# Earlier column sums, grouped weight differences and earlier x transfers in a fused cross-attention and expert layer

## The chip, the cores and the metric

The kernel runs on one core of one Trainium2 chip. The metric is device time in microseconds (us); a run that the measurement labels slow is kept out of every comparison. Engines are named as in the profile: PE (TensorE, matmuls), DVE (VectorE), ACT (ScalarE), POOL (GpSimd) and SP (SyncE, which issues transfers). Starts and landings are counted from the start of the profiled span.

## The reference

Eight batches, each of 8 heads, 512 rows of x and 32 rows of state with 64 columns, go through a cross attention in both directions; the 544 x 512 result of a batch goes through a two-layer network with 2048 hidden columns.

```python
scores = x @ state^T / 8;   a  = softmax(scores);   xread = a @ state
scores2 = state @ x^T / 8;  a2 = softmax(scores2);  sread = a2 @ x
y = concatenate([xread, sread], rows)          # heads side by side: 4352 x 512
h = y @ w_in                                   # 4352 x 2048
r = maximum(h, 0);  g = s * r*r + b            # s and b are single numbers
out = g @ w_out                                # 4352 x 512
```

## The kernel before

Step s of the main loop computes the hidden layer of batch s in 16 pieces f, and between them the output matmuls of batch s-1, the attention of batch s+1 and the transfers for later batches. In the names of the code and the profile, h is the hidden layer before its relu and g after its square, o (or oA, oB, oC by bank) the output, T the scores from the transposed x, xT that transpose, wsum the column sums; qa and u are what DVE reads out of banks A and B, and osb is a finished block of output. The output of batches 1 to 7 is made by a seven-product scheme in half-size blocks: its products read differences of weight blocks (`wd`) and sums of token blocks (`s`), and collect in three banks A, B and C. The constant b enters as b times the column sums of w_out; these sums are made once, in step 1.

```python
def bias_sum():                                  # column sums of w_out
    ps = att_ps([P, DM], FP32, "wsum_ps")
    ...                                          # 16 matmuls in tiles of 32 columns
    nc.vector.tensor_copy(wsum[:, 0], ps)
    nc.vector.tensor_sub(wsum[:, 1], ps, wsum[:, 0])

def bias_end():                                  # PE reads wsum here
    for i in range(2):
        mm(ps2, mean16, wsum[:, i], start=(i == 0), stop=(i == 1))
    ...

# the order of the seven products of the last batch: (product, from step, to step)
if b == last_b:
    order = [(1, 0, 8), (6, 0, 4), (2, 0, 2), (6, 4, 8), (2, 2, 5)]
    order += [(7, 0, 8), (2, 5, 8), (4, 0, 8)]
...
if s == 1:                                       # what step 1 does beside its matmuls
    ...
    at(8, lambda: att_xT_dma(3))                 # transpose of x of batch 3, by transfer
    at(12, lambda: load_x(4))
    at(3, bias_sum)                              # after the fourth h
    at(4, bias_end)
    ...
if 2 < s < B - 2:
    at(0, lambda: load_x(s + 2))
...
for f in range(NKF):
    mm1_x(s, f)                                  # the h of piece f: 2 matmuls, relu, square
    ...
    for fn in todo_s.get(f, []):
        fn()
    if (s == 1 and 5 <= f < 12) or (s == 2 and f == 6):
        with tc.issue_after(G["last"]):
            sums.pop(0)()                        # one weight difference
```

PE, SP and POOL run in the order written; DVE and ACT are scheduled. The transpose of batch 3 stands in a chain of transfers: the load of x of batch 3 waits on POOL for the transpose of batch 2, and the transpose of batch 3 waits for that load.

The softmax here doesn't subtract the row's maximum and nothing guards it: scores larger than these inputs give would overflow.

Of the kernel before, what the change touches and what calls it, by code (L numbers as in the profile page):

```python
# [14 lines left out]
def kernel(  # L15
# [15 lines left out]
    B, H, S, D = x.shape  # L31
# [81 lines left out]
    def new_xn(b):  # L113
        xn[b] = xpool.tile([P, H, SCH, D], FP16, name=f"xn_{b}", tag="xn", bufs=5)
# [3 lines left out]
    def load_x(b):  # L118
        new_xn(b)
        nc.gpsimd.dma_start(  # L120
            out=xn[b].rearrange("p h c d -> p h (c d)"),
            in_=x[b].rearrange("h (q c) d -> q h (c d)", q=P),
        )
# [48 lines left out]
    def new_xT(b):  # L172
        A[b]["xT"] = apool.tile([P, H, 2, P], FP16, name=f"xT_{b}", tag="xT")
        return A[b]["xT"]
# [27 lines left out]
    def att_xT_dma(b):  # L202
        xT = new_xT(b)
        nc.sync.dma_start_transpose(
            out=xT.rearrange("p h k t -> p (h k) t"),
            in_=xn[b].rearrange("p h c d -> p (h c d)"),
        )
# [46 lines left out]
    def att_shares(b):  # L254
        a = A[b]
        by_slot = "p j (q s) -> p (j q) s"
        den = apool.tile([P, NG * SCH * NQ], FP32, name=f"den_{b}", tag="den", bufs=1)
        inv = apool.tile([P, NG * SCH * NQ], FP16, name=f"inv_{b}", tag="inv", bufs=1)
        a["aT"] = apool.tile([P, NG * SCH, P], FP16, name=f"aT_{b}", tag="R", bufs=1)
        ET_s = a["ET"].rearrange(by_slot, q=NQ)  # L260
        with tc.issue_after(G["last"]):
            nc.vector.reduce_sum(den, ET_s, axis=mybir.AxisListType.X)
            with nc.allow_low_precision("shares are fp16"):
                nc.vector.reciprocal(inv, den)
            nc.vector.tensor_mul(
                a["aT"].rearrange(by_slot, q=NQ),
                ET_s,
                inv.unsqueeze(2).broadcast_to([P, NG * SCH * NQ, Ns]),
            )

    def att_a4_dma(b):
        a = A[b]
        a["a4"] = apool.tile([P, NG, S], FP16, name=f"a4_{b}", tag="a4")
        nc.sync.dma_start_transpose(
            out=a["a4"].rearrange("p g (c t) -> p (g c) t", c=SCH),
            in_=a["aT"].rearrange("t j p -> t (j p)"),
        )
# [27 lines left out]
    def att_ET(b):  # L305
        a = A[b]
        a["ET"] = apool.tile([P, NG * SCH, P], FP16, name=f"ET_{b}", tag="ET", bufs=3)
        nc.sync.dma_start_transpose(out=a["ET"], in_=a["E"].rearrange("p g t -> p (g t)"))
        a["rq"] = apool.tile([P, NG], FP32, name=f"rq_{b}", tag="rq", bufs=4)
        nc.vector.reciprocal(a["rq"], a["rs"])  # L310
# [41 lines left out]
    def mm1_open(key, ntok, f):  # L352
        pool, tag = psH, "h"
        if key == 0 and f % 2 == 1:
            pool, tag = (psA, "att") if f < 8 else (psH, "h")
        return pool.tile([P, ntok], FP32, tag=tag, name=f"h_{key}_{f}")
# [17 lines left out]
    def mm1_k(b, f, g, hps):  # L374
        a = A[b]
        mm(
            hps,
            a["M"][:, g, P * f : P * f + P],
            a["a4"][:, g, :],
            start=(g == 0),  # L380
            stop=(g == NG - 1),
        )

    def mm1_x(b, f):
        hps = mm1_open(b, S, f)
        for g in range(NG):
            mm1_k(b, f, g, hps)
        mm1_close(b, hps, S, f)
# [86 lines left out]
    def fast_items(b):  # L475
# [119 lines left out]
        order = [(1, 0, 8), (6, 0, 4), (2, 0, 3), (6, 4, 8), (2, 3, 8), (7, 0, 8)]  # L595
        order += [(5, 0, 8), (4, 0, 8), (3, 0, 8)]
        if b == last_b:
            order = [(1, 0, 8), (6, 0, 4), (2, 0, 2), (6, 4, 8), (2, 2, 5)]
            order += [(7, 0, 8), (2, 5, 8), (4, 0, 8)]
        if b == "sr":  # L600
            order = [(p, 0, 8) for p in (1, 6, 2, 7, 5, 4, 3)]
        out = [(p, k, i) for p, k0, k1 in order for k in range(k0, k1) for i in range(ni)]
# [57 lines left out]
    with tc.manual_schedule(engines={ET.PE, ET.SP, ET.Pool}):  # L660
# [90 lines left out]
        def pieces(s):  # L751
            nb = s + 1
            out = {}

            def at(f, fn):
                out.setdefault(f, []).append(fn)

            if s == 1:
                at(0, lambda: att_xT_dma(2))
                at(0, gated_x3)  # L760
                at(0, lambda: att_ET(0))
                at(0, lambda: att_ET(1))
                at(8, lambda: att_xT_dma(3))
                at(12, lambda: load_x(4))
                at(2, lambda: att_M(1, 2, "act"))
                at(3, bias_sum)
                at(4, bias_end)
                at(3, lambda: att_M(1, 3, "act"))
                at(6, lambda: att_stT(2))
                at(10, bias_half)  # L770
                at(8, lambda: att_M(2, 0, "act"))
                at(8, lambda: att_M(2, 1, "act"))
                at(10, lambda: att_M(2, 2, "act"))
                at(10, lambda: att_T(2, [0, 1]))
                at(11, lambda: att_ET(2))
                at(12, lambda: att_D(2, [0, 1]))
                at(13, lambda: att_M(2, 3, "act"))
                at(13, lambda: att_V(0))
                return out
            if 2 < s < B - 2:  # L780
                at(0, lambda: load_x(s + 2))
            if nb < NST:
                at(0, lambda: att_stT(nb))
            if nb < B:
                at(3, lambda: att_T(nb, [0, 1]))
                at(3, lambda: att_M(nb, 0, "act"))
                at(4, lambda: att_ET(nb))
                at(8, lambda: att_shares(nb))
                at(9, lambda: att_a4_dma(nb))
                if s == 3:  # L790
                    at(9, stT_dma)
                if nb + 1 < B:
                    at(9, lambda: att_xT_dma(nb + 1))
                at(7, lambda: att_M(nb, 1, "act"))
                at(7, lambda: att_M(nb, 2, "act"))
            if s == 2:
                at(1, lambda: att_srT_dma(0))
                at(8, lambda: att_V(1))
                at(12, lambda: att_srT_dma(1))
            at(10, lambda: att_V(s))  # L800
            if s == last_b:
                at(11, lambda: att_srT(s))
            else:
                at(12, lambda: att_srT_dma(s))
            if nb < B:
                at(10, lambda: att_M(nb, 3, "act"))
            if s == last_b:
                for i in range(4):
                    at(12 + i, lambda i=i: mm1_sr(i))
            return out  # L810
# [4 lines left out]
        for s in range(1, B):  # L815
            todo_s = pieces(s)
            if s in fast:
                coming[s] = fast_items(s)
            first = coming[s][:16] if s in fast else []
            if s == 1:  # L820
                items = [[] for _ in range(NKF)]
                for f in [*range(5), *range(6, 14)]:
                    items[f] = [lambda u=todo.pop(0): unit(u)]
                items[14], items[15] = first[0:8], first[8:16]
            else:
                flat = coming[s - 1][16:] + first
                n = -(-len(flat) // NKF)
                items = [flat[n * f : n * f + n] for f in range(NKF)]
            for f in range(NKF):
                mm1_x(s, f)  # L830
                if s > 1 and f in (5, 6):
                    with tc.issue_after(G["last"]):
                        token_sum(s - 1, 4, f - 5)
                if s in fast:
                    if f in ((7, 9) if s == 1 else (7, 11)):
                        with tc.issue_after(G["last"]):
                            token_sum(s, 3, f // 8)
                    if s == 1 and f in (13, 14):
                        with tc.issue_after(G["last"]):
                            token_sum(s, f - 12, 0)  # L840
                    if s > 1 and f in (11, 12):
                        token_sum(s, f - 10, 0)
                    if f == 15:
                        token_sum(s, 1, 1)
                        token_sum(s, 2, 1)
                for fn in todo_s.get(f, []):
                    fn()
                if (s == 1 and 5 <= f < 12) or (s == 2 and f == 6):
                    with tc.issue_after(G["last"]):
                        sums.pop(0)()  # L850
                for fn in items[f]:
                    fn()
# [56 lines left out]
```

## Time and profile before

| | before |
|---|---|
| time, median of three runs (lowest to highest) | 209.89 us (209.81 to 210.26) |
| span of the profiled run | 207.7 us |
| first output matmul of batch 0 starts | 23.18 us |
| T of batch 3 (scores from transposed x) starts | 56.78 us |
| last matmul starts | 203.64 us |
| transpose of x of batch 3 lands | 55.43 us |

The table cuts the span into an **opening** (23.18 us, loads and first attention), a **first stretch** up to the T of batch 3 (56.78-23.18 = 33.60), a **second stretch** up to the last matmul (203.64-56.78 = 146.86), and some 4.1 us in which the last results are read out and stored. PE leads throughout the two stretches.

### The profile page before, as it was taken

To read this page: it belongs to the slowest core of one execution; us is meant where nothing else is said; L and a number is where in the kernel's file an instruction comes from. 1 tells how busy PE (TensorE), PEld (TensorE's weight loads), DVE (VectorE), ACT (ScalarE), POOL (GpSimd) and SP (SyncE) were. 2 spreads that over 40 slices of the span, in tenths; PEclk is the share of its full clock that TensorE was granted. 3 is DMA by queue.
4 is the path that set the end of the run, shared out by engine and by line. 5 is a ranking of instruction groups with operands and counts; after the bars stand their busy time and mean duration, and the time that the engine had idled before them with its cause. 6 is when DMAs were issued, how large, how long until landed. Compare 5 with 4: busy or idle time off the path is not lost.

```text
span 207.7 us, 4765 instructions
## 1 busy us (share of the span) xinstructions
PE 199.8 (96%) x1949; PEld 129.6 (62%) x1949; DVE 162.2 (78%) x286; ACT 123.4 (59%) x216; POOL 37.6 (18%) x64
## 2 busy tenths in 40 slices
PE   7988999999999999999999999999999999999992
PEld 2424343445666676667666766676667777788881
DVE  1587825978779995999699968996899787796862
ACT  3678865698477548755776477656774545533100
POOL 5970001411110230023012201120112012100210
PEclk9999999999999999999999999999999999999999
DMA  6999996999750589269943983291314111200143
GB/s 181 227 202 206 206 192 91 192 172 180 208 67 37 125 197 133 68 78 241 141 96 96 213 110 101 80 192 44 101 58 103 50 54 50 97 7 0 55 148 106
DMA packets 46490, 25.48 MB, mean 123 GB/s; under 512 B 31428, under 2 KB 44484, under 8 KB 46468
## 3 DMA queue, kind: packets, MB, share of 16 engines
q0 software_dynamic: 15536, 16.19, 38.4%
q1 hardware_dynamic: 30132, 8.62, 23.5%
q10 hardware_dynamic: 800, 0.36, 0.7%
q8 instruction: 15, 0.25, 0.5%
q14 instruction: 7, 0.06, 0.1%
HBM read 17.33 MB, written 8.91 MB: 126 GB/s over the span
## 4 chain that ended last, share of the span: by engine, by line
PE 84%; DVE 8%; ACT 4%; issue 1%; DVEq 0%
PE h L70 23%; PE oB L70 16%; PE oC L70 11%; PE oA L70 11%; PE o L70 6%; PE Mps L70 4%; PE warm_ps L70 3%; PE h_sr L70 3%; ACT r L365 2%; DVE g L371 2%; PE T L70 1%; PE oB_sr L70 1%; PE V L70 1%; DVE M L298 1%; PE oC_sr L70 1%
## 5 line engine op out<-in xcount | busy, mean ns | idle before, releaser
L365 ACT ACTIVATE r<-h 128x512 f16<-128x512 f32 x126 | 74.5, 601 | 54.1 <-PE h L70 53.4
L70 PE MATMUL h<-a,M 128*128 128x512 f16 x256 | 75.0, 379 | 0.9 <-DVE M L298 0.6
L371 DVE TENSOR_TENSOR g<-r 128x1024 f16<-128x1024 f16 x64 | 44.1, 691 | 21.2 <-ACT r L365 21.0
L70 PEld LDWEIGHTS <-s 128*128 128x128 f16 x448 | 42.8, 98 | 19.2 <-issue 4.2
L70 PEld LDWEIGHTS <-g 128*128 128x128 f16 x400 | 38.1, 98 | 18.9 <-issue 2.9
L536 POOL DMA_DIRECT2D out_dram<-osb x27 | 18.3, 676 | 124.4 <-DVE osb L528 123.1
L70 PE MATMUL oB<-wd,s 128*128 128x256 f16 x224 | 32.7, 273 | 0.0
L70 PE MATMUL oA<-wo,g 128*128 128x256 f16 x224 | 31.7, 273 | 0.1
L70 PEld LDWEIGHTS <-M 128*128 128x128 f16 x256 | 24.6, 98 | 10.8 <-DVE M L298 1.6
L301 ACT CAST M<-Mps 128x1024 f16<-128x1024 f32 x27 | 26.8, 1016 | 1.4 <-PE Mps L70 0.8
L70 PE MATMUL oC<-wd,s 128*128 128x256 f16 x112 | 16.5, 273 | 0.0
L70 PE MATMUL o<-wo,g 128*128 128x512 f16 x64 | 16.3, 380 | 0.0
L70 PE MATMUL oB<-wd,g 128*128 128x256 f16 x112 | 15.9, 273 | 0.0
L70 PE MATMUL oC<-wo,s 128*128 128x256 f16 x112 | 15.3, 272 | 0.4 <-DVE osb L528 0.4
L365 ACT ACTIVATE r_sr<-h_sr 128x256 f16<-128x256 f32 x16 | 6.1, 382 | 8.4 <-PE h_sr L70 8.4
L471 DVE TENSOR_TENSOR s<-s,g 128x1024 f16<-128x1024 f16 x14 | 9.6, 689 | 0.3
L227 ACT ACTIVATE E<-T 128x512 f16<-128x512 f32 x16 | 9.4, 596 | 0.5 <-PE T L70 0.4
L70 PE MATMUL h_sr<-srdT,wi 128*128 128x256 f16 x64 | 9.6, 273 | 0.0
L465 DVE TENSOR_TENSOR s<-g 128x1024 f16<-128x1024 f16 x14 | 9.6, 684 | 0.0
L469 DVE TENSOR_TENSOR s<-g,g 128x1024 f16<-128x1024 f16 x14 | 9.6, 683 | 0.0
L473 DVE TENSOR_TENSOR s<-g,s 128x1024 f16<-128x1024 f16 x14 | 9.1, 684 | 0.0
L528 DVE SCALAR_TENSOR_TENSOR osb<-oC,s_bc,u 128x512 f32<-128x512 f32 x12 | 8.6, 714 | 0.0
(102 smaller groups left out, 188.4 us busy)
## 6 DMA issues: line engine op xcount, KB each, us to landing
out_dram<-osb POOLq DMA_DIRECT2D x31, 256.0 KB, 3.1
xn<-in_x_dram POOLq DMA_DIRECT2D x7, 512.0 KB, 8.1
wi<-in_moe_w_in_dram POOLq DMA_DIRECT2D x4, 512.0 KB, 8.5
wo<-in_moe_w_out_dram POOLq DMA_DIRECT2D x4, 512.0 KB, 16.2
xf<-in_x_dram SPq DMA_DIRECT2D x2, 512.0 KB, 4.7
out_dram<-osb_sr SPq DMA_DIRECT2D x8, 32.0 KB, 1.5
out_dram<-osb_sr ACTq DMA_DIRECT2D x8, 32.0 KB, 1.7
out_dram<-osb_last SPq DMA_DIRECT2D x2, 128.0 KB, 2.0
```

The costliest lines, as they stand in the source:

```text
L70: return nc.tensor.matmul(out, lhsT, rhs, start=start, stop=stop, tile_position=tp, is_transpose=is_transpose, skip_group_check=True,)
L227: nc.scalar.activation(a["E"][:, g, :].rearrange("p (m t) -> p m t", m=2), T[:, :, 256 * i : 256 * i + 256], AF.Exp, scale=scale, accum_ou ...
L298: nc.vector.tensor_copy(dst[:, 0], two[0])
L301: nc.scalar.copy(dst, ps)
L365: nc.scalar.activation(r16[:, f % 2], hps, AF.Relu)
L371: nc.vector.tensor_mul(gt[:, f % 4 - 1 : f % 4 + 1], r16, r16)
L465: nc.vector.tensor_sub(o, a11, a21)
L469: nc.vector.tensor_add(o, a21, a22)
L471: nc.vector.tensor_sub(o, SQ[b, 1, j], a11)
L473: nc.vector.tensor_sub(o, a12, SQ[b, 2, j])
L528: nc.vector.scalar_tensor_tensor(osb, acc[bank], s_bc, add, ALU.mult, ALU.add)
L536: nc.gpsimd.dma_start(dst[j][:, :, n0 : n0 + NH], osb)
```

## The change

Four things move: the column sums go in front of the fourth h instead of behind it; all eight weight differences are made in step 1; the last batch's second product runs four steps before the sixth resumes; x loads and transposes are issued about one batch sooner.

```diff
         if b == last_b:
-            order = [(1, 0, 8), (6, 0, 4), (2, 0, 2), (6, 4, 8), (2, 2, 5)]
+            order = [(1, 0, 8), (6, 0, 4), (2, 0, 4), (6, 4, 8), (2, 4, 5)]
...
+            def ahead(f, fn):
+                out.setdefault((f, "ahead"), []).append(fn)
...
-                at(3, bias_sum)
+                ahead(3, bias_sum)
...
-            if 2 < s < B - 2:
-                at(0, lambda: load_x(s + 2))
+            if s == 2:
+                at(1, lambda: load_x(5))
+            elif s in (3, 4):
+                at(1, lambda: load_x(s + 3))
...
+                if s in (2, 3):
+                    at(6, lambda: att_xT_dma(nb + 1))
                 at(9, lambda: att_a4_dma(nb))
-                if s == 3:
+                if s == 2:
                     at(9, stT_dma)
-                if nb + 1 < B:
-                    at(9, lambda: att_xT_dma(nb + 1))
+                elif s in (3, 4):
+                    at(9, lambda: att_xT_dma(s + 3))
...
             for f in range(NKF):
+                for fn in todo_s.get((f, "ahead"), []):
+                    fn()
                 mm1_x(s, f)
...
-                if (s == 1 and 5 <= f < 12) or (s == 2 and f == 6):
+                if s == 1 and 5 <= f < 13:
```

## The prediction

> **What bounds the kernel now.** I read the page first, then the waits of PE, then the timelines of PE and DVE around each wait, and last the landings of the transfers.
>
> ```profile
> PE 199.8 (96%) x1949; PEld 129.6 (62%) x1949; DVE 162.2 (78%) x286; ACT 123.4 (59%) x216; POOL 37.6 (18%) x64
> ...
> PE h L70 <- DVE M L298: 0.6, 1, 0.6
> PE T L70 <- ACT xT L197: 0.4, 1, 0.4
> PE oC L70 <- DVE osb L528: 0.4, 1, 0.4
> ```
>
> PE is busy for 96% of the span, so a gain can only come from PE's idle time or from fewer matmuls. The change keeps the number of matmuls. From 24 us on, the waits of PE name only two or three short events. A PE row's end is modelled, so I take stalls from starts instead: a 512-column matmul takes 0.216 us to the next start and a 256-column one 0.109 us (eight oA rows in 0.87 us). Rows of the PE timeline, in order of time:
>
> ```profile
> 33.26 1.04 PE L70 MATMUL o<-wo,g 128*128 128x512 f16 x4
> 34.13 0.59 PE L70 MATMUL h<-a,M 128*128 128x512 f16 x2
> 35.02 0.61 PE L70 MATMUL bias_ps<-wsum,mean 128*128 128x512 f16 x2 [0.29 <-DVE wsum L621]
> ...
> 68.85 0.49 PE L70 MATMUL oB<-wd,g 128*128 128x256 f16 x3
> 69.72 0.60 PE L70 MATMUL oC<-wo,s 128*128 128x256 f16 x4 [0.38 <-DVE osb L528]
> ...
> 182.95 0.49 PE L70 MATMUL oB<-wd,s 128*128 128x256 f16 x3
> 183.50 0.38 PE L70 MATMUL oA<-wo,g 128*128 128x256 f16 x2
> ```
>
> The reader is to see start plus count times spacing against the next start: 34.13+0.43=34.56 against 35.02 (0.46 us lost, **stall A**), 68.85+0.33=69.18 against 69.72 (0.54, **stall B**), 182.95+0.33=183.28 against 183.50 (0.22). By the same reckoning there are two of 0.16 us, at 55.3 (oB waits for a token sum) and 191.6 (oB waits for the u read of its bank). These five, some 1.55 us, are nearly all that waiting costs after the first 24 us, and batches 3 to 6 have none. The first 24 us are not touched by the change. So the ceiling of any reordering here is about 1.5 us in 209.89, 0.7%.
>
> **What the Trainium skill says.** "TensorE: Matmul & The Clock Gate", section Back-to-back issue gap, gives about N/2.4+2.5 ns per isolated matmul: 216 ns at 512 columns and 109 at 256, which are this trace's spacings. "Perfetto Trace Analysis", section Identifying the Most-Contended Engine, warns that matmul busy share is no good measure of headroom: here the idle brackets show 0.29 and 0.38 us where the starts show 0.46 and 0.54. "DMA: Bandwidth & Descriptors", section Queues, rings and completion order, says that each DMA engine takes turns between the rings it has work for, and takes one ring in order: the trace agrees in that a transpose of x took 4.4 us alone (34.60 to 39.01) and 9.1 us beside loads and stores (46.30 to 55.43). "SBUF — State Buffer", section Who interferes with whom, says a DVE instruction with two SBUF inputs contends with a GpSimd one that reads SBUF: the g at 32.67 took 0.96 us instead of 0.69, under a POOL copy from 32.26 to 33.09.
>
> **The change part by part.** The instruction orders of both kernels show the same instructions in other places.
>
> 1. *Weight column sums ahead of the fourth h.* Stall A's chain is on DVE:
>
> ```profile
> 32.67 0.96 DVE L371 TENSOR_TENSOR g<-r 128x1024 f16<-128x1024 f16 x1 [2.34 <-ACT r L365]
> 33.55 0.68 DVE L620 CAST wsum<-wsum_ps 128x512 f16<-128x512 f32 x1
> 34.27 0.69 DVE L621 TENSOR_TENSOR wsum<-wsum_ps,wsum 128x512 f16<-128x512 f32 x1
> ```
>
> The sums finished about 32.82, but the g stood before their cast. Now the sums start at 31.50 (o ends 31.41, plus 0.09 for going from full array to tiles, as the 31.63 h to 31.95 wsum shows), end at 32.37, and DVE, idle then, casts at 32.57 (0.20 us from matmul end to DVE, as in oC to osb_last at the end), subtracts at 33.29 and is done at 33.98; the g comes after. PE meanwhile: back to full array 0.10, h 0.43, to tiles 0.09, Mps 0.35, o 0.87, h 0.43, and reaches the bias matmul at 34.66. No wait is left; one more switch of tile mode costs 0.10. **Gain 35.02-34.66 = 0.36.** The last weights, which the sums read, landed at 30.59, 0.9 us before.
>
> 2. *All weight differences in batch 1.* One DVE subtraction moves from 62.41 to behind the one at 47.14. There it costs nothing: 0.15 us of idle lie before 47.89 and 0.59 before the a at 49.23, which waits for ACT, against 0.60 for the subtraction. Where it leaves, DVE is without a pause up to the osb that releases stall B:
>
> ```profile
> 61.21 1.29 DVE L473 TENSOR_TENSOR s<-g,s 128x1024 f16<-128x1024 f16 x2
> 62.41 0.69 DVE L455 TENSOR_TENSOR wd<-wo,wd 128x1024 f16<-128x1024 f16 x1
> 63.01 0.74 DVE L562 SCALAR_TENSOR_TENSOR u<-oB,s_bc,qa 128x512 f32<-128x512 f32 x1
> ...
> 68.92 0.74 DVE L528 SCALAR_TENSOR_TENSOR osb<-oC,s_bc,u 128x512 f32<-128x512 f32 x1
> ```
>
> Each one's input is there 0.6 us sooner (oB is done at 61.62, the r for the g at 62.96 and 66.47), so the osb starts at 68.32 and frees the bank by 69.1, against PE's 69.18. **Gain 0.54**, give or take 0.05.
>
> 3. *The last batch's order*, in the diff though not in its summary: piece 2 runs four steps instead of two before piece 6 resumes, and one instead of three after it. Eight oB matmuls move later, so piece 6 ends at 186.56 instead of 185.69. Piece 7 adds to the same bank and must wait for DVE to read it: u starts at 186.56+0.20=186.76, takes 0.74, so piece 7 starts at 187.55 instead of 187.21. In exchange the token sum gets 0.9 us more, which it did not need: ready at 184.10, used at 184.37. The 0.22 at 183.3 waits for qa and stays. **Loss 0.34.**
>
> 4. *x loads and transposes a batch sooner.* PE never waits for them in batches 2 to 7: the transpose used at 79.16 landed at 76.32. Later ones lie alike. Hidden before, hidden after: **0**.
>
> Sum: -0.36-0.54+0.34 = **-0.56 us**, so 209.33, say 209.3.
>
> **The rivals.** *A transfer becomes the bound.* The load of x for batch 5 now starts at about 53 us, while the transpose for batch 3 is in flight; that landed at 55.43, PE needs it at 56.78 (56.42 after part 1). If it is over 1 us later, part of the gains is lost, total about 209.9. For it: 9.1 us beside other traffic. Against it: the load stands behind an output store (52.46 to 56.91) on its own ring. One in six.
>
> *The wait moves and nothing is gained.* PE that arrives sooner could meet the same DVE later, at the 0.16 us stall at 55.3 or in batch 3. Against: DVE has idle time by ACT or PE before each (0.59 at 49.23, 1.49 at 57.52), so it moves along with PE. Would make 209.7 to 209.9.
>
> *Part 3 costs nothing or helps.* If DVE reads the bank sooner, or the qa stall shrinks, the whole gain of 0.9 shows: 209.0. For it: whoever made the change meant it to help. Against: the arithmetic above.
>
> *The earlier traffic helps.* Batches 5 to 7 get their x sooner and the late windows carry less, but no PE wait there is for it to take.
>
> **Range and chances.** The three runs before spread 0.45 us, as much as the effect. With 0.3 us for the terms and 0.3 for the runs, 208.8 to 209.9 should hold it eight times in ten. Over 2% would need 4.2 us, three times all stalls: faster 0.01. Slower by 4.2 us would need a new wait in every batch from the transposes: 0.01. Within 2%: 0.98.
>
> **What the profile after would show.** Part 1: no wait on wsum, the bias matmul at about 34.7, the g behind the subtraction. Part 2: no idle bracket before the first oC of batch 2 on wo, and it starts 0.9 us sooner, near 68.8. Part 3: piece 7's first oB in the tail about 0.3 us behind the oA before it, waiting on u. Part 4: transposes land sooner, with PE unmoved. I am wrong if the transpose for batch 3 lands after 56.4, if the last weights land after 31.5 so that the sums wait, or if the tail has no new gap.

## The result, and the profile after

| | before | after |
|---|---|---|
| median, four runs each on one chip | 209.86 | 209.94 |
| lowest to highest | 209.81 to 210.26 | 209.29 to 210.02 |
| ratio of fast runs, 95% interval | | 0.9993 (0.9970 to 1.0016) |

A ratio here is the mean time of one kernel's fast runs over that of the other's of the same rounds, so it is not quite the ratio of the medians. By the ratio the change is worth 0.0007 x 209.9 = 0.15 us, where 0.56 was predicted; the median rose by 0.08. All is far inside 2%.

First the points at which the prediction said what would show it right. These are the PE timeline's rows of the changed kernel (start, modelled length, instruction, count, idle time before it); a 512-column matmul takes 0.216 us to the next start, a 256-column one 0.109:

```profile
33.24 0.61 PE L70 MATMUL h<-a,M 128*128 128x512 f16 x2
...
34.99 0.59 PE L70 MATMUL h<-a,M 128*128 128x512 f16 x2
35.42 0.59 PE L70 MATMUL bias_ps<-wsum,mean 128*128 128x512 f16 x2
...
69.25 0.49 PE L70 MATMUL oB<-wd,g 128*128 128x256 f16 x3
69.57 0.60 PE L70 MATMUL oC<-wo,s 128*128 128x256 f16 x4
...
186.96 0.27 PE L70 MATMUL oA<-wo,g 128*128 128x256 f16 x1
187.42 0.60 PE L70 MATMUL oB<-wd,s 128*128 128x256 f16 x4 [0.19 <-DVE u L557]
```

34.99+0.43 = 35.42: stall A is gone. 69.25+0.33 = 69.58 against 69.57: stall B is gone. 186.96+0.11 = 187.07 against 187.42: a new gap of 0.35 us in the tail, waiting for u, where 0.34 was predicted. The DVE timeline of the changed kernel shows the sums ahead of the g, as foreseen:

```profile
33.36 0.69 DVE L620 CAST wsum<-wsum_ps 128x512 f16<-128x512 f32 x1 [2.27 <-PE wsum_ps L70]
34.09 0.69 DVE L621 TENSOR_TENSOR wsum<-wsum_ps,wsum 128x512 f16<-128x512 f32 x1
34.70 0.68 DVE L371 TENSOR_TENSOR g<-r 128x1024 f16<-128x1024 f16 x1
```

The traffic has moved too. This is the page's row of GB/s by fortieths of the span (5.2 us each), before and then after:

```profile
GB/s 181 227 202 206 206 192 91 192 172 180 208 67 37 125 197 133 68 78 241 141 96 96 213 110 101 80 192 44 101 58 103 50 54 50 97 7 0 55 148 106
```

```profile
GB/s 183 223 202 206 206 192 102 180 172 161 236 142 134 155 135 133 160 79 234 122 81 96 217 7 98 91 105 19 101 71 90 50 54 50 101 3 0 55 148 106
```

In the eleventh to thirteenth slices, 52 to 67 us, 208, 67 and 37 have become 236, 142 and 134: the load of x of batch 5 and what follows it now run there. No wait of PE on a transfer comes of it in this run; the transpose of batch 3 lands at 55.32 and is used at 57.18.

So every part did what it was to do, and yet the span went from 207.7 to 207.9 us. What is left is the opening. The PE timeline before, at its first transposes and its first output matmul:

```profile
5.63 0.61 PE L70 MATMUL xTps<-ident,xn 128*128 128x128 f16 x8
6.08 0.27 PE L70 MATMUL stTps<-ident,st 128*128 128x128 f16 x2
...
22.06 1.28 PE L70 MATMUL h<-a,M 128*128 128x512 f16 x4
23.18 1.89 PE L70 MATMUL o<-wo,g 128*128 128x512 f16 x8
```

and the same places after:

```profile
5.86 1.06 PE L70 MATMUL xTps<-ident,xn 128*128 128x128 f16 x8
6.96 0.28 PE L70 MATMUL stTps<-ident,st 128*128 128x128 f16 x2
...
22.82 1.28 PE L70 MATMUL h<-a,M 128*128 128x512 f16 x4
23.94 1.89 PE L70 MATMUL o<-wo,g 128*128 128x512 f16 x8
```

The program is the same up to here, and it is 0.76 us later. The eight transposes of x take 0.45 us until those of the state start, and 1.10 after. PE's clock records show full clock from 5.38 us before and from 6.81 after; the first part of the state landed at 5.49 and at 6.46. From the first output matmul to the last matmul it is 180.46 us before and 179.91 after: **-0.55 us**, against the predicted -0.56. The opening took back 0.76.

### The profile page after: what moved, and what is told of

Read it like the earlier page. It is cut to its first block, busy times and chain, and to the rows that moved or that the text cites. A ratio compares the mean times of both kernels' runs of the same rounds, so it can differ in the third digit from the quotient of the medians.

```text
span 207.9 us, 4764 instructions
## 1 busy us (share of the span) xinstructions
PE 200.4 (96%) x1949; PEld 130.0 (63%) x1949; DVE 162.2 (78%) x286; ACT 123.3 (59%) x216; POOL 38.0 (18%) x64
## 4 chain that ended last, share of the span: by engine, by line
PE 88%; DVE 4%; DMA 3%; ACT 2%; POOL 1%; issue 0%; ACTq 0%
PE h L70 25%; PE oB L70 18%; PE oC L70 12%; PE oA L70 11%; PE o L70 7%; PE Mps L70 4%; DMA stf<-in_state_dram 3%; PE h_sr L70 3%; ACT r L365 2%; PE T L70 1%; PE V L70 1%; PE oB_sr L70 1%; DVE M L298 1%; PE oC_sr L70 1%; PE oA_sr L70 1%; DVE g L371 1%
```

## The experiments

All ratios are to the kernel before, run in the same rounds; by the 2% rule every verdict is "same". The expectations write "T of batch 2" for the T that runs in step 2; this is the T of batch 3 of this text, and their "mid part" is the time from the first output matmul to the last matmul.

Two theories to start with. The first: the opening is drawn anew in each run, whatever the kernel, and the parts are worth what the prediction says. The second: the change itself delays the opening, for example by another layout of the program or its memory. A third joined them: that PE, arriving sooner, meets a late transfer in some runs.

This table holds the profiled run of every kernel. "T wait" is the time by starts between PE being ready for the T of batch 3 and its start; the first stretch ends where PE is ready, the second begins with the T's start.

| kernel | opening | first stretch | transpose of batch 3 lands | T wait | second stretch |
|---|---|---|---|---|---|
| before | 23.18 | 33.60 | 55.43 | 0 | 146.86 |
| after | 23.94 | 33.24 | 55.32 | 0 | 146.66 |
| 1 after, again (labelled slow) | 22.92 | 33.26 | 58.15 | 2.02 | 148.33 |
| 2 after, old last order | 24.21 | 33.24 | 54.57 | 0 | 146.32 |
| 3 before, new last order | 23.90 | 33.34 | 54.59 | 0 | 147.20 |
| 4 before, x sooner | 23.09 | 33.61 | 54.84 | 0 | 146.86 |
| 5 before, sums and differences | 23.09 | 33.24 | 57.63 | 1.34 | 146.32 |
| 6 before, state first | 24.06 | 33.34 | 54.95 | 0 | 146.86 |
| 7 as 2, x of batch 5 earlier still (labelled slow) | 23.19 | 33.24 | 60.32 | 3.93 | 147.58 |
| 8 combined | 23.77 | 33.24 | 55.35 | 0 | 146.06 |
| 9 after, x of batch 4 later | 23.12 | 33.24 | 54.09 | 0 | 147.47 |
| 10 before, x of batch 4 later | 23.20 | 33.61 | 52.65 | 0 | 146.86 |
| 11 as 5, x of batch 4 later | 23.66 | 33.24 | 52.71 | 0 | 146.32 |
| 12 combined, x of batch 4 later | 23.66 | 33.24 | 52.69 | 0 | 146.04 |

### 1. The changed kernel again

No edit. It ran with experiments 2 to 4 beside eleven runs of the kernel before (median 210.18).

> The changed kernel once more. Theory T1 (chance in the opening): from the first output matmul of batch 0 (23.18 us before, 23.94 after) to the last matmul the changed kernel is 0.55 us shorter whatever happens, and the first output matmul itself starts anywhere between about 23.1 and 24.0, set by when the first part of state lands (5.49 us before, 6.46 after). So the span of this profile is 183.97 us plus that start, and the times are spread by some 0.8 us. Theory T2 (the change delays the opening): the first output matmul starts at 23.9 again and the state lands at about 6.4, in this and in every run with the change, and not in the kernels that share the opening of the kernel before.

Measured: 210.19 median of six (209.21 to 210.67 and one of 212.78 labelled slow), ratio 0.9990 (0.9967 to 1.0013), -0.21 us, much as in the first comparison. The profiled run is the one labelled slow, so its length settles nothing. But its opening, 22.92 us and over before the wait, is the earliest of all fourteen profiles, and a fast run with the whole change (experiment 9) opened at 23.12. **The second theory falls**: the change does not delay the opening each time. In the same run PE waits for the T of batch 3 (bracket: idle time and what ended it):

```profile
55.65 0.59 PE L70 MATMUL h<-a,M 128*128 128x512 f16 x2
58.20 0.44 PE L70 MATMUL T<-xT,stT 64*32 64x256 f16 x16 [1.95 <-DMA xT<-xn]
```

The trace's clock records then show PE at half clock from 58.83 to 62.24. The table of windows for that stretch has the clock in its third column from the right, 0.50:

```profile
58.80:62.20 3.40, 3.40 (x23) 2.05 (x16) 0.93 (x3) 2.70 (x6) 0.00 (x0) 0.50 1.54 199
```

3.41 us at half clock can cost up to 1.7 us of work, and in this one run the second stretch is 148.33-146.66 = 1.67 longer. As only runs labelled slow show it, nothing here rests on it. A wait of that kind had to be sought in a fast run: experiment 5.

### 2. Without the new last order

```diff
 # changed kernel
-            order = [(1, 0, 8), (6, 0, 4), (2, 0, 4), (6, 4, 8), (2, 4, 5)]
+            order = [(1, 0, 8), (6, 0, 4), (2, 0, 2), (6, 4, 8), (2, 2, 5)]
```

> The changed kernel with the old order of the last batch. If the new order costs 0.35 us (a gap of 0.35 us ahead of piece 7 in the tail of the changed kernel), this one is 0.35 us faster than the changed kernel, about 0.9 us shorter than the kernel before from the first output matmul of batch 0 to the last matmul: 180.46 before, 179.90 changed, 179.55 here. With openings alike the time is 209.0. Rival (the order was put in for a reason: the token sum is late without it): a new gap ahead of the second half of piece 6, near 184 us, and no gain.

Measured: 209.82, ratio 0.9983 (0.9967 to 0.9998), -0.36 us. In the trace the second stretch is 146.32, 0.34 shorter than in the changed kernel and 0.54 shorter than before: the loss of part 3 and the gain of part 2, each as predicted. The whole does not show it, for this profile has the latest opening of all, 24.21.

### 3. The new last order alone

```diff
 # kernel before
-            order = [(1, 0, 8), (6, 0, 4), (2, 0, 2), (6, 4, 8), (2, 2, 5)]
+            order = [(1, 0, 8), (6, 0, 4), (2, 0, 4), (6, 4, 8), (2, 4, 5)]
```

> The kernel before with only the new order of the last batch. If it costs 0.35: time 210.2, from first output matmul of batch 0 to the last matmul 180.81 against 180.46, with one new gap of 0.35 us near 187. Rival: no difference, 209.86. For the opening: T1 says that the state may land late here as well; T2 says that it lands early, as in the kernel before.

Measured: 210.55, ratio 1.0016 (1.0000 to 1.0033), **+0.34 us** (interval 0 to 0.69), and the second stretch is 147.20, 0.34 longer. The PE timeline of this kernel:

```profile
187.55 0.27 PE L70 MATMUL oA<-wo,g 128*128 128x256 f16 x1
188.01 0.60 PE L70 MATMUL oB<-wd,s 128*128 128x256 f16 x4 [0.19 <-DVE u L557]
```

The gap is 188.01-187.66 = 0.35 us, the same as in the changed kernel. One surprise lies in the first stretch: 33.34 instead of 33.60, with nothing moved there. DVE's timeline says why:

```profile
33.40 0.69 DVE L371 TENSOR_TENSOR g<-r 128x1024 f16<-128x1024 f16 x1 [2.34 <-ACT r L365]
34.01 0.68 DVE L620 CAST wsum<-wsum_ps 128x512 f16<-128x512 f32 x1
34.72 0.69 DVE L621 TENSOR_TENSOR wsum<-wsum_ps,wsum 128x512 f16<-128x512 f32 x1
```

The g took 0.69 us, where it took 0.96 before. The POOL copy that lay over it before, and the same copy here:

```profile
32.26 0.83 POOL L747 COPY st<-st 128x768 f16<-128x768 f16 x1 [16.94 <-DMA st<-in_state_dram]
```

```profile
32.16 0.83 POOL L747 COPY st<-st 128x768 f16<-128x768 f16 x1 [16.79 <-DMA st<-in_state_dram]
```

The copy waits for a transfer and not for PE, so it does not move with the opening. The opening is 0.72 us later, so the g starts after the copy has ended. All fourteen profiles agree: the g took 0.96 to 0.97 us in the three where the copy lies over it, and 0.68 to 0.69 in the other eleven. **Stall A is 0.46 us with an early opening and 0.19 with a late one**, so part 1 is worth 0.36 or 0.10.

The opening itself: the state landed at 5.46 us, as before (5.49), but the clock records show full clock only from 7.20 us, against 5.38 before.

### 4. Only the earlier x

```diff
 # kernel before
-            if 2 < s < B - 2:
-                at(0, lambda: load_x(s + 2))
+            if s == 2:
+                at(1, lambda: load_x(5))
+            elif s in (3, 4):
+                at(1, lambda: load_x(s + 3))
 ...                        # and the transposes, as in the change
```

> The kernel before with only the earlier loads and transposes of x. My prediction: 0, the same 180.46 from the first output matmul of batch 0 to the last matmul, and 209.86 in time with openings alike. T2 needs this part to delay the opening (nothing else in the change touches transfers): first output matmul at 23.9 and some 210.6. A third way, the transpose of batch 3 lands after 56.8 because the load of batch 5 runs beside it: a gap ahead of T in batch 2.

Measured: 210.23, ratio 1.0004 (0.9983 to 1.0024). Both stretches are those of before to 0.01 us (33.61 and 146.86): **part 4 is worth 0**. The six runs fall in two groups, 209.74 to 209.88 and 210.57 to 210.65. Only one run is profiled, of the shorter group, and it opened early; that the other group opened late is likely and not shown.

### 5. Column sums and weight differences alone

```diff
 # kernel before
-                at(3, bias_sum)
+                ahead(3, bias_sum)
 ...
-                if (s == 1 and 5 <= f < 12) or (s == 2 and f == 6):
+                if s == 1 and 5 <= f < 13:
```

> Parts 1 and 2 alone: the column sums ahead, all weight differences in batch 1, with the loads of x and the last batch as before. From the first output matmul of batch 0 to the last matmul: 180.46 before; with stalls A (0.46 less one switch of 0.10) and B (0.54) gone 179.56, the same as with the earlier x and without the new last order (179.56 measured), if the earlier x is worth nothing. Time 0.9 us under the kernel before in the mean, the opening adding its spread of about 1.3 us to single runs. Rival (the earlier x is what took stall B or A away): 180.0 or more.

Measured, beside eleven runs of before on another chip (210.31): 210.02, ratio 0.9982 (0.9970 to 0.9993), -0.38 us, where parts 1 and 2 add up to -0.90. This profiled run is a fast one with an early opening, and it waits:

```profile
55.80 0.59 PE L70 MATMUL h<-a,M 128*128 128x512 f16 x2
57.67 0.44 PE L70 MATMUL T<-xT,stT 64*32 64x256 f16 x16 [1.27 <-DMA xT<-xn]
```

By the starts PE was ready at 56.33, as 23.09+33.24 says, and the transpose landed at 57.63, so 1.34 us are lost, more than the gain of 0.90. Its two stretches are otherwise the best ones, 33.24 and 146.32. The kernel has none of the earlier x traffic, so that traffic is not needed for the wait. Only here do the third theory and the numbers meet: an **early** opening plus parts 1 and 2 brings PE to this T at 56.2 to 56.4 us, and the transpose's landing follows the chain of transfers instead. That chain starts at the same time in all kernels: the x of batch 2 landed at 34.2 to 34.6 us in every profile.

### 6. The state's transfer first

```diff
 # kernel before
         nc.vector.memset(warm, 0.0)
+        nc.scalar.dma_start(stf[:, 0:2, :], st_v[:, 0:2, :])
         nc.scalar.dma_start(ident16, ident_dr.ap())
 ...
-        nc.scalar.dma_start(stf[:, 0:2, :], st_v[:, 0:2, :])
```

The state's first part had landed at 5.49 us before and at 6.46 after; this was to make the opening early each time.

> The kernel before with one edit in the opening: the first part of state is issued on the ACT queue ahead of the identity, 0.4 us sooner. Theory: the opening waits for the later of two things, the landing of that part (5.1 to 6.7 us in six profiles) and the moment when the TensorE clock goes up (4.2 to 7.2 us). Then the state lands about 0.5 us or more sooner, the first T no longer starts past 6.8 because of it, and the median falls by 0.1 to 0.4 us; runs where the clock comes late stay late (first output matmul 23.9), so the spread does not vanish. Rival: the landing does not depend on the order of issue and nothing changes.

Measured: 210.31, ratio 0.9992 (0.9979 to 1.0005): **a miss**. The state landed at 4.71, but the identity, now second on the same queue, at 6.07 instead of 3.08, and the first transposes need it. The opening is 24.06. The identity and full clock, from 6.98 us, both came late.

### 7. The x of batch 5 earlier still

This doubles the suspected traffic beside the transpose of batch 3.

```diff
 # kernel of experiment 2
                 at(13, lambda: att_V(0))
+                at(13, lambda: load_x(5))
                 return out
-            if s == 2:
-                at(1, lambda: load_x(5))
-            elif s in (3, 4):
+            if s in (3, 4):
                 at(1, lambda: load_x(s + 3))
```

> The changed kernel with the old last order and the load of x for batch 5 moved forward again, to the end of batch 1, so that its data go ahead of an output store and beside the transpose of batch 3. If an x load in flight beside that transpose can make T of batch 2 wait: the transpose lands at 57 or later in place of 54.6, T waits 0.5 us or more in the profile, and the time is 0.5 to 2 us above the one with the load in batch 2 (209.82). Rival: the transpose lands as before and the time is the same; then the late landing of 58.15 in one run of the changed kernel had another cause.

Measured: 209.51 to 212.03 in four fast runs and two of 214.1 labelled slow; ratio of the fast ones 0.9997 (0.9959 to 1.0035). The transpose took 11.20 us (49.12 to 60.32) in the profiled run, which is a slow one, and the T waited:

```profile
55.91 0.59 PE L70 MATMUL h<-a,M 128*128 128x512 f16 x2
60.36 0.65 PE L70 MATMUL T<-xT,stT 64*32 64x256 f16 x16 [3.86 <-DMA xT<-xn]
```

The wait is at the same place as in experiment 5, and longer; again the clock halved after it (59.69 to 63.11). The landing was as expected in the one profile. The expected 0.5 to 2 us on the time is **not shown**: the fast runs of this kernel are 0.9997 of before and those of experiment 2, on another chip, 0.9983, with intervals that overlap. That fast runs of one kernel range over 2.5 us would fit a wait in some of them, but they were not profiled.

### 8. Parts 1 and 2 with a mended tail

The trace before left a wait of 0.22 us for qa in the tail and, at 191.6, one of 0.16 for u. Here the reads of the banks go ahead of the token sums on DVE. The state goes first, x is as before.

```diff
 # kernel of experiment 5, with the state's transfer first
             if p == 1:
                 ...
+                if b == last_b:
+                    with tc.issue_after(nc.cur_bb.bb.instructions[-1]):
+                        token_sum(b, 1, 1)
+                    token_sum(b, 2, 1)
 ...
-                    if f == 15:
+                    if f == 15 and s != last_b:
 ...
-            if f in (11, 12, 13):
-                token_sum("sr", (1, 2, 4)[f - 11], 0)
+            if f in (11, 13):
+                token_sum("sr", {11: 1, 13: 4}[f], 0)
             go(rest, 5)
+            if f == 12:
+                with tc.issue_after(G["u3", last_b]):
+                    token_sum("sr", 2, 0)
```

> Parts 1 and 2, no earlier x, the old last order, state first, and two DVE orders in the tail: qa ahead of the token sum before it (the 0.22 us stall at 183.3), and the u that frees bank B ahead of a token sum of the state rows (the 0.16 us stall at 191.6). From the first output matmul of batch 0 to the last matmul: 179.56-0.22-0.16=179.18. Time about 1.3 us under the kernel before plus what state first gives, so 208.5 to 208.9 where the kernel before takes 210. If the token sum that goes back is late instead, a new gap of up to 0.3 us stands ahead of the second half of piece 6 and most of the 0.22 is lost.

Measured: 209.26 (209.18 to 209.34), ratio **0.9948** (0.9936 to 0.9960), -1.1 us. The second stretch is 146.06, 0.26 below that of experiment 5; the two waits together gave 0.38 to gain. What remains of the one for qa shows under experiment 12. By both stretches the gain is 1.16 us, less than the 1.3 expected. State first gave nothing here either: the identity landed at 6.17 us and the first transposes waited for it, though full clock came at 5.27, and the opening is 23.77.

### 9 to 11. The x of batch 4 later

If the load of x of batch 4, issued at about 41.3 us and landing at about 52, is what holds the transpose of batch 3 up, then issuing it later must bring the landing forward and take the wait away. Three kernels, beside eleven runs of before (210.19).

```diff
 # 9: changed kernel; in 10 and 11, the kernel before and that of experiment 5,
 # only the load of batch 4 moves to step 2
-                at(12, lambda: load_x(4))
 ...
             if s == 2:
-                at(1, lambda: load_x(5))
+                at(1, lambda: load_x(4))
+                at(8, lambda: load_x(5))
```

> The changed kernel with one edit: the load of x for batch 4, issued at 41.3 us until now and moving its data between 46 and 52 us beside the transpose of batch 3, is issued in batch 2 instead (and that of batch 5 behind it). Theory (the race): T of batch 2 starts at the later of two moments, the first output matmul of batch 0 plus 33.2 us, and the landing of the transpose of batch 3, which ten profiles put anywhere from 54.6 to 60.3; the gains of parts 1 and 2 are lost where the opening is early and the landing late. Then the transpose lands at 53 or sooner here, T never waits, every run has the gain of 0.56 us, and the ratio to the kernel before is 0.997 with a smaller spread than 209.2 to 212.8. Rival (the transpose is late for another reason than the load beside it, or the opening is late by the change): it lands at 55 or later, the ratio stays at 0.999.

> The kernel before with the same edit. There T of batch 2 is reached at 56.7 or later (first output matmul plus 33.5), when the transpose had landed in all profiles of kernels with the old column sums. Theory: the transpose lands at 53 or sooner, but nobody waited for it: ratio 1.000 within 0.001, mid part 180.46. Rival: the edit is a gain by itself, 0.998 or less.

> Parts 1 and 2 with the same edit. Without it they gave 0.9982, half of their 0.9 us, and the profile had T waiting 1.34 us. Theory: the mid part is 179.56 in the profile, whatever the opening, and the ratio is 0.9957. Rival: 0.998 again.

Measured: the transpose took 5.37 us (48.72 to 54.09), 6.36 and 5.61 instead of 9.91, 9.13 and 8.97 in experiment 1, before and experiment 5. Experiment 10 against before is the clean pair: both opened at 23.2, the input of the transpose landed at 46.15 and 46.17, and only the load of batch 4 moved. **So this load is a cause of the slow transpose**, by 2.8 us there, and no T waits in any of the three. The packets say how: in before, the transpose issued at 46.30 moved its first packet at 49.36, and until then only packets of POOL's queue ran; in experiment 10 it took from 46.29 to 47.47.

Experiment 9 (which moves the load of batch 5 too) shows that this takes the wait away: it opened early (23.12), PE was ready at 56.36, and the transpose, whose input landed as late as in experiment 5 (48.58 against 48.53), was there. That late input is the other half of the wait and stays open: it landed at 48.1 to 49.0 in the early-opening kernels with the sums ahead, and at 48.06 in the profiled run of after, against 46.2 to 46.6 in the early-opening kernels with the sums in their old place and 46.5 to 47.3 in the other late-opening ones.

Experiment 9 trades the wait for another, in the PE timeline of batch 3:

```profile
73.21 0.93 PE L70 MATMUL oA<-wo,g 128*128 128x256 f16 x7
74.77 0.61 PE L70 MATMUL h<-a,M 128*128 128x512 f16 x2 [0.63 <-DMA a<-aT]
```

Seven matmuls take 0.76, so 0.80 us are lost, and the second stretch is 147.47 instead of 146.66. PE now waits for the transpose of the attention result, which was issued at 69.28 and landed at 74.72; in the changed kernel it was issued at 68.28 and took 3.7 us instead of 5.4. That the later loads crowd it is likely and not shown. The ratio is 0.9989 (0.9972 to 1.0005), where 0.997 was expected: **a miss**, as the one wait went and another came.

The profiled run of experiment 10 has the stretches of before to 0.01 us, and still the ratio is 0.9984 (0.9967 to 1.0000), where 1.000 within 0.001 was expected. **That -0.34 us does not show in the stretches of the one profile; it is taken here as a measure of how far the times of a few runs can be off**, though a gain in the unprofiled runs is not excluded. Experiment 11 has 33.24 and 146.32 and no wait, as expected; its ratio is 0.9975 (0.9953 to 0.9998), -0.5 us, where 0.9957 was expected, with runs from 208.86 to 210.28, and why some took 210.28 is open.

### 12. The mended tail with x of batch 4 later

As experiment 8, without the state's transfer first and with x of batch 4 later.

```diff
 # kernel of experiment 8, identity first as before
-                at(12, lambda: load_x(4))
 ...
             if s == 2:
+                at(1, lambda: load_x(4))
```

> Parts 1 and 2, the old last order, the two DVE orders of the tail (qa and u ahead of token sums), the load of x for batch 4 late, and the opening as before (state first put the identity at 6.1 us and gained nothing). Mid part 179.3, as in the profile of the best so far, or 179.2. That one had the first output matmul at 23.77 because the identity came late; with 23.1 to 23.9 here the time is 208.6 to 209.4 and the ratio 0.993 to 0.994. Rival: an early opening makes another transfer late and the time stays at 209.3.

Measured: 209.27 (209.03 to 209.93), ratio **0.9954** (0.9937 to 0.9971), -1.0 us. In its PE timeline the wait for qa is nearly gone:

```profile
183.07 0.60 PE L70 MATMUL h_sr<-srdT,wi 128*128 128x256 f16 x4
183.51 0.38 PE L70 MATMUL oA<-wo,g 128*128 128x256 f16 x2
183.81 0.50 PE L70 MATMUL oB<-wd,s 128*128 128x256 f16 x3
```

183.51+0.22 = 183.73 against 183.81, 0.08 us left. By both stretches the gain is 1.18 us; the ratio came out just short of the 0.993 to 0.994 expected. Experiments 8 and 12 are faster than the kernel before by about 1 us, and the only ones whose gain lies well outside what experiment 10 shows of the noise. The changed kernel was not run beside them; in its own two comparisons it took 209.94 and 210.19.

## Why the prediction was right or wrong

**Part 1, right with an early opening.** Predicted -0.36; the first stretch is 33.24 against 33.60. (The terms listed for PE add up to 34.64, not the 34.66 written; by the trace after it is 34.66, counted from the same opening.) But stall A was taken as fixed at 0.46. With a late opening the g meets no POOL copy, the first stretch of the unchanged order is 33.34, and the part is worth 0.10. The prediction had quoted the collision and not asked whether it comes in each run.

**Part 2, right.** Predicted -0.54; the second stretch of experiment 2 is 146.32 against 146.86.

**Part 3, right.** Predicted +0.34; +0.34 in both stretches that tell it (experiments 2 and 3), and +0.34 in time. The interval of the last is 0 to 0.69, so that its close agreement is in part luck.

**Part 4, right.** Predicted 0; experiment 4 has both stretches unchanged.

**The sum, right in the trace and short in the time.** -0.55 between the first output matmul and the last matmul, -0.15 in the mean (interval -0.63 to +0.34), and the median 209.94 lies just above the range's end of 209.9. The step that failed is the sentence "The first 24 us are not touched by the change" and the term of zero that it stood for. They are not touched, but they are not constant: the first output matmul started between 22.92 and 24.21 us in the fourteen profiles, 1.3 us apart and more than twice the effect. The profiled run of before was among the early ones and that of after among the late. Each of the seven late openings (23.66 and later) has at least one of two things, or, in experiments 6 and 8 with their edited opening, a late identity; none of the seven early ones (23.20 and earlier) has any. One is the moment when PE's clock goes to full, from 3.94 us (experiment 5) to 7.20 (experiment 3) and past 6.2 in five of the late ones, though PE was busy from 1.2 us on in every one. The other is the landing of the first part of the state, mostly 5.1 to 5.5 us (4.7 in experiments 6 and 8, where it goes first) but 6.46 in the changed kernel, 6.73 in experiment 2 and 6.17 in experiment 11. "TensorE: Matmul & The Clock Gate" of the Trainium skill, section What you observe, puts the transition at about 4 us into sustained work, give or take half a microsecond from run to run; that it varies agrees, the width seen here is larger than this figure. Half of the 1.3 us, about 0.6, would have been a fitter allowance for the runs than 0.3 (an estimate).

**The rival "a transfer becomes the bound", right in the wait and wrong in its cause.** It named the transpose of batch 3, a need at 56.42 and the x of batch 5. The wait came, in a fast run, in a kernel without the earlier x of batch 5 (experiment 5), and the load that held the transpose up is that of batch 4, which both kernels have (experiments 9 to 11), on top of an input that landed 2 us late for a reason that is open. The margin of 56.78-55.43 = 1.35 us was read from one run; over the profiles with that load in its old place and nothing added the landing ranges from 54.57 to 58.15. So the change loses something in either case: opened late, part 1 has less to take away; opened early, it can run into the transpose. The prediction also took the 9.1 us of that transpose as agreeing with rings that take turns; for the first 3.06 of them the packets show no turn of the transpose's ring at all. Parts 1 and 2 without part 3 gave -0.36 and -0.38 us in experiments 2 and 5, both intervals short of -0.90.

**What stays open.** The unprofiled runs tell no opening and no wait, so how much of the missing 0.4 us each of the three takes (later openings, the smaller stall A, the wait for the transpose) is not measured; and by its interval the comparison of four runs does not exclude the full 0.56. Whether the change makes late openings more or less frequent, fourteen profiles of different kernels cannot tell. The half clock after waits of 2.0 us and more was seen only in two runs labelled slow.

## What to carry to other kernels

When a kernel is at 96% on one engine, cut the trace at fixed instructions and compare stretch by stretch: here that gave each part to some hundredths of a microsecond, while whole times could hardly tell 0.3. Before a sum of small gains is trusted, look at which events hang on the bound engine and which on transfers that start at a fixed time: an earlier arrival at the first kind is a gain, at the second it may turn into a wait, and a margin read from one run is not a margin. Ask too what varies before the part that is changed, for a start-up that differs by a microsecond from run to run hides a gain of half of one.

## What the Trainium skill lacked or had wrong

- "TensorE: Matmul & The Clock Gate", section What you observe: the transition to full speed is given as around 4 us into sustained activity, within half a microsecond. Here PE was busy from 1.2 us on and full clock came between 3.94 and 7.20 us of the span, so 2.8 to 6.0 us into it, in fourteen profiles; the half microsecond is too narrow. (The page's next section, with counts of 6, 11 and 14 slow matmuls in one kernel, leaves room for more.)
- The same page, section Why this matters for your kernels, asks for no PE-idle gaps over about 3 us. In two runs, both labelled slow, waits of 2.02 and 3.93 us were followed by half clock for 3.41 us each time, so the first gap was shorter than the page's figure; after a wait of 1.34 us, in a fast run, the clock stayed full. The window of 3413 ns in the page's section What's actually happening agrees with the length.
- "DMA: Bandwidth & Descriptors", section Latency and other measured facts, gives 261 GB/s for a transpose by transfer and no figure beside other traffic. The 512 KB transpose of x took 4.41 us from issue to landing with only smaller transposes behind it on its queue; 1.28 of them passed before its first packet, and the first 512 KB on the queue then moved in 2.53 us (35.88 to 38.41), 207 GB/s. Beside stores it took 5.4 to 6.4 us, beside stores and the load of batch 4 it took 7.1 to 9.9, and 11.2 with the load of batch 5 issued right behind it as well.
- "SBUF — State Buffer", section Who interferes with whom, has the rule right and no size for this case: the g took 0.96 us under a POOL copy and 0.69 without (three and eleven profiles), and whether the two meet changes with the opening.
- No page says that a clock read from the profile's records is unknown before the first record: in the run of before the tables of windows used here show 1.00 from 1.5 to 4.0 us, though the first record of full clock is at 5.38 and 512-column matmuls are 0.427 us apart there.
